# Weight preparation in an attention and expert-layer kernel: two sums drawn in the next chunk, squares drawn four places later

## The chip, the cores and the metric

The kernel runs on one core of one Trainium2 chip. The metric is the device time of one execution in microseconds (us). Before the change, three timed runs took 1914.98, 1915.31 and 1919.73 us; the median is 1915.31 us.

## The reference

Three layers follow one another; all inputs and the result are 32-bit in the reference, apart from what is noted below.

```python
# attention: 4 x 8 heads, 576 positions, head size 64, window 128
scores = q @ k.T / 8 + bias                  # bias = -slope_h * |i - j|, masked outside the window
x = softmax(scores) @ v                      # -> 2304 tokens x 512

# experts: 8 experts, 512 -> 1024 -> 512
P = exp(x @ w_gate - max)
for _ in range(8):                           # alternate row and column normalisation
    P /= P.sum(1, keepdims=True) + 1e-09
    P /= P.sum(0, keepdims=True) + 1e-09
    P *= 2304 / 8
x = sum(P[:, e:e+1] * (relu(x @ w1[e]) @ w2[e]) for e in range(8))

# last layer: 512 -> 2048 -> 512
h = x @ w_in                                 # w_in and w_out come as 64-bit floats
out = maximum(0.01 * h, h) @ w_out
```

## The kernel before

**Chunks and pairs.** Both expert layer and last layer are cut into chunks of 512 hidden columns: 16 chunks of the experts (0 to 15, two for each expert) and 4 of the last layer (16 to 19). The tokens are 18 tiles of 128, grouped into five pairs of token blocks (pairs 0 to 3 of two tiles a side, pair 4 of one). A unit is one chunk and one pair. From chunk 1 to chunk 18 the units of a chunk run in the order of pairs 0, 4, 1, 2, 3.

**Products.** A 2 x 2 block product is formed with seven products instead of eight (the list `PRODUCTS`), each of 16-bit high and low halves. A step is one such product: six matmuls of 256 columns (twelve of 128 for pair 4's first product). The first product of a unit (`a_steps`, matmuls at L728, "a") makes hidden values: ACT copies results out of the accumulation banks (L740, L752), DVE adds (L744, L757), ACT rounds to 16 bits (L776, L782, L798) and POOL forms the low halves (L801). The second product (`b_steps`, matmuls at L845, "b") takes them one unit later and adds onto the output tiles: DVE in one instruction (L858), or for two of the seven products ACT (L855) followed by POOL (L856). In the loop at L1031 the "a" steps of a unit are merged with the "b" steps of the unit before.

**Weights.** While a chunk runs, the weights of the next are prepared. `Weights` (L562) has one object for the first weights (`which` 0) and one for the second (`which` 1). `load` fetches 1024 KB on SP's queue into a buffer `raw`, of which there are two. `scale` squares the four quarters on ACT (L576, with sums), finds a power of two from them by small DVE and PE instructions (`scale_jobs`, L406), and scales the quarters on ACT (L579); for the second weights `back` (L588) follows. `part` (L605) splits a quarter into two 16-bit halves with ACT (L446) and POOL (L447). `sums` (L596) makes four sums and differences of quarters on POOL (L603). Parts 0 and 1 are taken before the sums; parts 2 to 6 need them (6 the third, 4 the fourth) and are made step by step in the last seven steps of the last "a" unit of a chunk (first weights) or of the "b" steps after it (second weights), by `at` (L621).

**Conversions.** In chunks 1 to 11 the list also holds the turning of the last layer's 64-bit weights into 32-bit ones, three conversions a chunk in chunks 1 to 10 and two in chunk 11 (`to_single`, L635). A conversion loads 512 KB into a `raw` buffer, and has five jobs: exponent (L657 DVE, L660 ACT), signed (L663 DVE), high (L668 DVE, L669 ACT), low (L675 ACT, L677 POOL) and put (L681 POOL, then a write of 256 KB, L682). The two `raw` buffers are taken in turn: first conversion, second conversion, first weights, third conversion, second weights. So the load of the first weights waits for the first conversion's write, and that of the second weights for the third conversion's write.

**The side list.** `side_jobs` (L1000) makes the list of these jobs for the next chunk; `None` is an empty place. It is begun with the unit of pair 4. After every step `tick` (L137) draws jobs from its head, as many as `-(-len(side) // max(len(seq) - k + rest, 1))` at step k, with `rest` 57, 36, 8 and -19 in the units of pairs 4, 1, 2 and 3. With the list of 85 jobs of a chunk with three conversions that is two jobs in each of the first seven steps and then one, and the list is empty before the end of pair 3. In pair 0's unit one job is drawn a step.

**What sets the order.** Jobs are drawn inside `tc.issue_after(...)` for each of the `anchors`: on its own engine a job's instruction must come behind the last evacuation that was recorded for that engine by the steps so far (`anchor`, L124). For the rest the planner of the tile framework (`schedule_with_timeline_sim=True`) orders the instructions of each engine ahead of time by place in the program and by when it takes their inputs to be there; on the chip each engine runs its own list in that order, and waits where an input is not there yet.

Of the kernel before, what the change touches and what calls it, by code (L numbers as in the profile page):

```python
# [31 lines left out]
def attn_moe_kernel(  # L32
# [80 lines left out]
    side, gating, inputs = [], [], []  # L113
# [337 lines left out]
    def weigh_pair(ci, p):  # L451
        t0, n = PAIRS[p]
        if ci not in pu:
            pu[ci] = small.tile([P, NTILE], F32, tag="pu", name="pu")
        c = slice(t0, t0 + 2 * n)
        nc.scalar.activation(out=pu[ci][:, c], in_=rxt[0 if ci == 0 else 1][:, c], func=AF.Copy, scale=rw[ci])

    class Inputs:
# [22 lines left out]
        def weigh(self):  # L481
            c = slice(self.t0, self.t0 + 2 * self.n)
            nc.scalar.activation(out=rxt[self.phase][:, c], in_=self.sr[:, 1:2].to_broadcast([P, 2 * self.n]), func=AF.Copy)
            if self.phase == 0:
                weigh_pair(0, self.p)
# [73 lines left out]
    W = [{}, {}]  # L559
    nw = [0, 0]  # L560

    class Weights:  # L562
# [52 lines left out]

        def early(self):
            if XTRA >= 2:
                return [lambda: self.part(0), lambda: self.part(1)] + [lambda k=k: self.sums(k) for k in range(4)]
            return []

        def at(self, j):  # L621
# [9 lines left out]
    def weights(ci):  # L631
        for which in range(2):
            W[which][ci] = Weights(ci, which)
# [366 lines left out]
    def side_jobs(ci, n):  # L1000

        todo = [to_single(cast.pop(0)) for _ in range(min(n, len(cast)))]
        weights(ci)
        a, b = W[0][ci], W[1][ci]
        jobs = [load for load, _ in todo[:2]]
        if not todo:
            return [a.load, b.load] + [None] * 10 + a.scale() + a.early() + b.scale() + b.early()
        jobs += [None] * 8 + todo[0][1] + [a.load]
        if len(todo) > 1:
            jobs += todo[1][1]  # L1010
        if len(todo) > 2:
            jobs += [todo[2][0]] + [None] * 4 + a.scale() + todo[2][1] + [b.load] + a.early()
        else:
            jobs += [b.load] + [None] * 8 + a.scale() + a.early()
        return jobs + [None] * 8 + b.scale() + b.early()
# [15 lines left out]
    for n, u in enumerate(units + [None]):  # L1031
        a, b = [], b_steps(*prev)
        if u == LAST:
            held_back = b[7:]
            b = b[:7]
        if u is None:
            b = held_back[:3] + [f for two in zip(b, held_back[3:] + [None] * 3) for f in two if f is not None]
        if u is not None:
            ci, p = u
            assert ci < NCE or p in split_pairs  # L1040
            a = a_steps(ci, p)
            k0 = len(a) - 7
            if p == ends[ci] and ci + 1 < NC:
                a = [[f] + ([lambda j=k - k0: W[0][ci + 1].at(j)] if k >= k0 else []) for k, f in enumerate(a)]
            else:
                a = [[f] for f in a]
        if prev[1] == ends[prev[0]] and prev[0] + 1 < NC:
            k0 = len(b) - 7
            b = [[f] + ([lambda j=k - k0: W[1][prev[0] + 1].at(j)] if k >= k0 else []) for k, f in enumerate(b)]
        else:  # L1050
            b = [[f] for f in b]
        if u is not None and ci >= 1:
            if n and units[n - 1][0] != ci and ci != NCE:
                weigh(ci)
            if p == 4:
                side += side_jobs(ci + 1, 3 if ci < NCE - 1 else 0) if ci + 1 < NC else []
        if prev[0] == NCE:
# [64 lines left out]
```

## Time and profile before

| What | Value |
|---|---|
| Median of three timed runs | 1915.31 us |
| The profiled execution | 1917.65 us |
| Its span | 1915.9 us |
| PE matmul busy | 1851.2 us (97%) |
| PE weight loads busy | 1609.8 us (84%) |
| ACT, POOL, DVE busy | 1363.5, 1325.1, 1312.1 us (71, 69, 68%) |
| DMA | 97.80 MB, nearly all on one queue (q1) |
| Load of 1024 KB of weights, median from issue to landing | 5.2 us |

PE multiplies, PEld loads its weights beside it, DVE, ACT and POOL are the other computing engines, SP issues the transfers. A row of the timeline gives the start in us, the duration in us, the engine, the line, the operation, what it writes and reads, its shape, and in brackets how long the engine was idle before it and what ended that. An idle time of an engine costs only when PE, or the end, waits for it.

### The profile page before, as it was taken

What the parts mean: (1) busy time and instruction counts of PE and PEld (TensorE: products, weight loads), DVE (VectorE), ACT (ScalarE), POOL (GpSimd) and SP (SyncE); (2) the same over time, 40 slices, a digit from 0 to 9 for tenths busy, and PEclk for the clock granted to TensorE, in tenths of its full rate; (3) what the DMA queues carried; (4) which work ended last, traced back from release to release, by engine and by line L of the source; (5) the groups of instructions that cost most, each with busy time, mean ns of one, the idle gap of its engine ahead of it and who ended that gap; (6) DMA issues with size and microseconds to landing.
All of it is one profiled execution on the core that took longest, in us unless ns stands there. A gap on an engine that the chain in (4) does not pass through costs nothing.

```text
span 1915.9 us, 45130 instructions
## 1 busy us (share of the span) xinstructions
PE 1851.2 (97%) x17725; PEld 1609.8 (84%) x17725; DVE 1312.1 (68%) x3608; ACT 1363.5 (71%) x3123; POOL 1325.1 (69%) x1140
## 2 busy tenths in 40 slices
PE   7899898999999999999999999999999998999999
PEld 5677787888888888988888888988889787889888
DVE  5455567766776767767676777666666687677877
ACT  7978767776767767676776767666665779776754
POOL 3843566877868686877868787685867786666753
PEclk8999999999999999999999999999999999999999
DMA  7522002021111202112111201100001010101002
GB/s 231 171 89 84 2 12 83 29 67 56 51 57 40 78 23 79 38 58 67 40 56 40 83 23 56 45 24 23 24 24 45 1 36 11 34 13 45 2 26 75
DMA packets 60453, 97.80 MB, mean 51 GB/s; under 512 B 3920, under 2 KB 26960, under 8 KB 60240
## 3 DMA queue, kind: packets, MB, share of 16 engines
q1 hardware_dynamic: 60240, 94.93, 15.4%
q8 instruction: 138, 2.26, 0.5%
q14 instruction: 75, 0.61, 0.1%
HBM read 81.81 MB, written 13.11 MB: 50 GB/s over the span
## 4 chain that ended last, share of the span: by engine, by line
PE 77%; ACT 10%; DMA 4%; DVE 4%; POOL 2%; issue 2%; SPq 0%; POOLq 0%; ACTq 0%; DVEq 0%
PE t L845 36%; PE s L728 21%; PE sq L728 15%; DMA raw<-in_moe_w_dram 3%; ACT e L261 2%; ACT junk L576 2%; PE o L305 1%; ACT raw L579 1%; PE pt L288 1%; DVE s L757 1%; ACT w L446 1%; PE s L249 1%; POOL h L801 1%; ACT xp L446 1%; ACT pb L292 1%
## 5 line engine op out<-in xcount | busy, mean ns | idle before, releaser
L845 PE MATMUL t<-w,h 128*128 128x256 f16 x7560 | 977.8, 273 | 15.1 <-DVE acc L858 5.3
L728 PEld LDWEIGHTS <-w 128*128 128x128 f16 x8400 | 758.5, 98 | 110.6 <-issue 28.6
L845 PEld LDWEIGHTS <-h 128*128 128x128 f16 x7560 | 729.5, 98 | 111.6 <-issue 24.2
L728 PE MATMUL s<-xp,w 128*128 128x256 f16 (+1 forms) x4872 | 611.6, 262 | 18.3 <-ACT q L752 11.4
L858 DVE SCALAR_TENSOR_TENSOR acc<-t,pu,acc 128x256 f32<-128x256 f32 x866 | 408.6, 478 | 207.9 <-PE t L845 160.0
L801 POOL TENSOR_TENSOR h<-s,h 128x1024 f16<-128x1024 f32 x180 | 389.0, 2161 | 120.1 <-ACT h L798 81.9
L728 PE MATMUL sq<-xp,w 128*128 128x256 f16 (+1 forms) x3528 | 451.1, 262 | 2.9 <-DVE s L757 2.6
L856 POOL TENSOR_TENSOR acc<-acc,part 128x256 f32<-128x256 f32 x322 | 234.7, 731 | 281.3 <-ACT part L855 246.4
L447 POOL TENSOR_TENSOR w<-raw,w 128x512 f16<-128x512 f32 x240 | 278.4, 1170 | 46.5 <-ACT w L446 46.2
L757 DVE SCALAR_TENSOR_TENSOR h<-sq,h 128x512 f16<-128x512 f32 (+1 forms) x352 | 192.8, 552 | 87.8 <-ACT h L782 49.3
L855 ACT ACTIVATE part<-t,pu 128x256 f32<-128x256 f32 x322 | 151.9, 472 | 100.8 <-PE t L845 95.1
L798 ACT ACTIVATE h<-s 128x1024 f16<-128x1024 f32 x180 | 189.7, 1054 | 43.4 <-DVE s L757 42.0
L744 DVE SCALAR_TENSOR_TENSOR sq<-sq,q 128x256 f32<-128x256 f32 x352 | 150.2, 427 | 60.3 <-PE sq L728 52.8
L740 ACT ACTIVATE q<-s 128x256 f32<-128x256 f32 x364 | 138.1, 381 | 70.3 <-PE s L728 57.1
L446 ACT ACTIVATE w<-raw 128x512 f16<-128x512 f32 x240 | 148.2, 628 | 8.9 <-PE t L845 6.6
L757 DVE SCALAR_TENSOR_TENSOR s<-sq,s 128x256 f32<-128x256 f32 x352 | 146.4, 416 | 2.0
L776 ACT ACTIVATE h<-sq 128x512 f16<-128x512 f32 x176 | 104.5, 594 | 59.3 <-PE t L845 30.1
L757 DVE SCALAR_TENSOR_TENSOR s<-sq,q 128x256 f32<-128x256 f32 x352 | 131.7, 415 | 13.4 <-ACT q L752 11.6
L744 DVE SCALAR_TENSOR_TENSOR sq<-s,q 128x256 f32<-128x256 f32 x176 | 75.4, 428 | 83.9 <-ACT q L740 78.8
L576 ACT ACTIVATE junk<-raw 128x512 bf16<-128x512 f32 x160 | 100.2, 626 | 44.2 <-DMA raw<-in_moe_w_dram 43.0
L782 ACT ACTIVATE h<-sq 128x256 f16<-128x256 f32 x176 | 66.8, 380 | 67.5 <-DVE sq L744 57.6
L579 ACT ACTIVATE raw<-raw,sr 128x512 f32<-128x512 f32 x160 | 102.4, 715 | 2.4 <-DVE sr L441 2.0
(142 smaller groups left out, 1713.0 us busy)
## 6 DMA issues: line engine op xcount, KB each, us to landing
raw<-in_moe_w_dram SPq DMA_DIRECT2D x32, 1024.0 KB, 5.2
k_t<-in_k_dram SPq DMA_DIRECT2D x16, 512.0 KB, 4.0
raw<-in_moe_w_in_dram SPq DMA_DIRECT2D x16, 512.0 KB, 3.6
raw<-in_moe_w_out_dram SPq DMA_DIRECT2D x16, 512.0 KB, 3.4
q_t<-in_q_dram SPq DMA_DIRECT2D x18, 256.0 KB, 4.1
v_t<-in_v_dram SPq DMA_DIRECT2D x18, 256.0 KB, 2.7
acc<-in_v_dram SPq DMA_DIRECT2D x18, 256.0 KB, 5.7
out_dram<-acc SPq DMA_DIRECT2D x36, 128.0 KB, 1.7
```

Source lines behind the costliest of these rows:

```text
L446: nc.scalar.activation(out=hi, in_=src, func=AF.Copy)
L447: return nc.gpsimd.tensor_tensor(out=lo, in0=src, in1=hi, op=ALU.subtract)
L576: nc.scalar.activation(out=junk, in_=self.raw[:, k], func=AF.Square, accum_out=self.mx[:, k:k + 1])
L728: nc.tensor.matmul(d[b][:, f, :], t[:, wp, kk, ft * P:(ft + 1) * P], XP[p][:, o, kk, xp, :], start=(i == 0 and f == 0 and j in FIRST), sto ...
L744: nc.vector.scalar_tensor_tensor(out=block(k), in0=ps, scalar=CS, in1=q[:, k], op0=ALU.mult, op1=ALU.add)
L757: nc.vector.scalar_tensor_tensor(out=out, in0=in0, scalar=sc, in1=in1, op0=op0, op1=op)
L798: nc.scalar.activation(out=h[:, 3:7, 0, :], in_=d["s"], func=AF.Copy)
L801: nc.gpsimd.tensor_tensor(out=h[:, 3:7, 1, :], in0=d["s"], in1=h[:, 3:7, 0, :], op=ALU.subtract)
L845: nc.tensor.matmul(ps, h[:, o, hp, f, tt * P:(tt + 1) * P], w[:, wp, ft, :], start=(i == 0 and j in FIRST), stop=(i == 5), skip_group_chec ...
L855: nc.scalar.activation(out=part, in_=ps, func=AF.Copy, scale=s)
L856: nc.gpsimd.tensor_tensor(out=dst, in0=dst, in1=part, op=ALU.add)
L858: nc.vector.scalar_tensor_tensor(out=dst, in0=ps, scalar=s, in1=dst, op0=ALU.mult, op1=ALU.add)
```

## The change

The third and fourth sums of the second weights leave the side list; they are put on the list anew at the unit of pair 0 of the chunk that uses these weights, behind one empty place each. And in a list with three conversions the empty places ahead of the first weights' `scale` (whose first jobs are the squares) are eight instead of four.

```diff
         def early(self):
             if XTRA >= 2:
-                return [lambda: self.part(0), lambda: self.part(1)] + [lambda k=k: self.sums(k) for k in range(4)]
+                return [lambda: self.part(0), lambda: self.part(1)] + [lambda k=k: self.sums(k) for k in range(4 - 2 * self.which)]
             return []
...
         if len(todo) > 2:
-            jobs += [todo[2][0]] + [None] * 4 + a.scale() + todo[2][1] + [b.load] + a.early()
+            jobs += [todo[2][0]] + [None] * 8 + a.scale() + todo[2][1] + [b.load] + a.early()
...
         if u is not None and ci >= 1:
             if n and units[n - 1][0] != ci and ci != NCE:
                 weigh(ci)
+            if p == 0:
+                side += [None, lambda w=W[1][ci]: w.sums(2), None, lambda w=W[1][ci]: w.sums(3)]
             if p == 4:
                 side += side_jobs(ci + 1, 3 if ci < NCE - 1 else 0) if ci + 1 < NC else []
```

## Rows read from the trace of the kernel before

**Rows 1.** The page, busy time, share of the span and instructions of each engine.
```profile
PE 1851.2 (97%) x17725; PEld 1609.8 (84%) x17725; DVE 1312.1 (68%) x3608; ACT 1363.5 (71%) x3123; POOL 1325.1 (69%) x1140
```

**Rows 2.** Stretches: length; PE, PEld, DVE, ACT, POOL busy; PE clock; DMA; GB/s.
```profile
347.20:1117.90 770.70, 758.41 (x7221) 670.77 (x7219) 546.80 (x1388) 544.10 (x1173) 591.04 (x496) 1.00 0.17 54
1117.90:1451.60 333.70, 333.70 (x3204) 297.62 (x3202) 221.66 (x586) 221.55 (x487) 239.12 (x204) 1.00 0.10 31
1451.60:1650.10 198.50, 185.75 (x1715) 159.37 (x1714) 140.56 (x391) 146.84 (x322) 140.79 (x115) 1.00 0.07 22
```

**Rows 3.** Waits over the span: who waited for whom, us, times, longest.
```profile
ACT junk L576 <- DMA raw<-in_moe_w_dram: 43.0, 22, 2.7
...
PE s L728 <- ACT q L752: 11.4, 13, 1.4
...
PE t L845 <- POOL h L801: 0.5, 2, 0.3
```

**Rows 4.** Timeline of chunk 9, around the first weights' load and squares.
```profile
981.40 0.86 DVE L858 SCALAR_TENSOR_TENSOR acc<-t,pu,acc 128x256 f32<-128x256 f32 x2
...
982.01 0.38 SPq L572 DMA_DIRECT2D raw<-in_moe_w_dram  x1
982.19 0.41 DVE L668 TENSOR_SCALAR raw<-raw 128x512 int32<-128x512 int32 x1
...
984.23 0.60 ACT L776 ACTIVATE h<-sq 128x512 f16<-128x512 f32 x1 [0.50 <-DVE sq L744]
...
987.20 0.63 ACT L576 ACTIVATE junk<-raw 128x512 bf16<-128x512 f32 x1 [2.38 <-DMA raw<-in_moe_w_dram]
...
989.82 0.38 ACT L752 ACTIVATE q<-s 128x256 f32<-128x256 f32 x1
...
990.25 1.70 PE L728 MATMUL s<-xp,w 128*128 128x256 f16 x12 [1.09 <-ACT q L752]
```

**Rows 5.** Timeline, ACT: the first squares in chunk 11 and in chunk 12.
```profile
1158.07 0.38 ACT L752 ACTIVATE q<-s 128x256 f32<-128x256 f32 x1
1160.05 0.63 ACT L576 ACTIVATE junk<-raw 128x512 bf16<-128x512 f32 x1 [1.60 <-DMA raw<-in_moe_w_dram]
...
1232.18 0.39 ACT L752 ACTIVATE q<-s 128x256 f32<-128x256 f32 x1
1232.45 0.64 ACT L576 ACTIVATE junk<-raw 128x512 bf16<-128x512 f32 x1
```

**Rows 6.** Timeline, POOL at the start of chunk 9: third and fourth sums, first later part.
```profile
952.60 1.28 POOL L603 TENSOR_TENSOR raw<-raw 128x512 f32<-128x512 f32 x1
953.83 1.43 POOL L856 TENSOR_TENSOR acc<-acc,part 128x256 f32<-128x256 f32 x2
955.20 1.29 POOL L603 TENSOR_TENSOR raw<-raw,t 128x512 f32<-128x512 f32 x1
...
962.26 1.16 POOL L447 TENSOR_TENSOR w<-t,w 128x512 f16<-128x512 f32 x1
```

**Rows 7.** Timeline of chunk 9: third conversion, second weights' load and first square.
```profile
1000.82 0.48 DVE L858 SCALAR_TENSOR_TENSOR acc<-t,pu,acc 128x256 f32<-128x256 f32 x1
...
1001.22 1.36 DVE L663 SCALAR_TENSOR_TENSOR raw<-raw,sign 128x512 int32<-128x512 int32 x1
...
1002.50 0.47 DVE L858 SCALAR_TENSOR_TENSOR acc<-t,pu,acc 128x256 f32<-128x256 f32 x1
...
1003.90 2.56 ACT L579 ACTIVATE raw<-raw,sr 128x512 f32<-128x512 f32 x4
...
1004.54 1.28 POOL L681 TENSOR_TENSOR raw<-raw 128x512 f32<-128x512 f32 x1
...
1007.95 0.38 SPq L572 DMA_DIRECT2D raw<-in_moe_w_dram  x1
...
1013.41 0.63 ACT L576 ACTIVATE junk<-raw 128x512 bf16<-128x512 f32 x1 [1.90 <-DMA raw<-in_moe_w_dram]
...
1014.04 0.36 ACT L740 ACTIVATE q<-sq 128x256 f32<-128x256 f32 x1
```

## The prediction, made before the changed kernel ran

> **What bounds the kernel now.** I read the busy line first: the matmul engine PE is busy 1851.2 of 1915.9 us, POOL, ACT and DVE about 70% of the span [rows 1]. So only PE's idle time, some 65 us, can be won, and anything new costs only what it makes PE wait. The table by stretches says where that idle time lies [rows 2]. In the nine chunks 2 to 10 (347.2 to 1117.9 us) PE is busy 758.41 of 770.70 us: 12.29 us idle, 1.37 us a chunk. In chunks 11 to 14 it is busy 333.70 of 333.70: nothing to win. In chunks 15 and 16, where the second layer's inputs are made, it is idle 198.50 - 185.75 = 12.75 us. The rest is attention, chunk 1 and the end. The granted clock is 1.00, the level of 2.4 GHz, in all three stretches, so it plays no part.
>
> Then the list of waits [rows 3]. PE's own largest is for ACT's copy L752: 11.4 us in 13 waits, at most 1.4. For POOL's h (L801) PE waits 0.5 us in the whole run: POOL is busy but no one that matters stands behind it. And ACT stands idle 43.0 us, 22 times, for a load of weights.
>
> The timeline of one chunk joins the two [rows 4]. The first weights' load is issued at 982.01. ACT finishes L776 at 984.83, and its next instruction in order is the first square (L576) of that load, which starts only at 987.20, when the load has landed, 5.19 us after its issue: ACT stands 2.38 us. Behind it are queued a copy of PE's product (L855), two more squares, L782 and L752; L752 runs at 989.82 and PE's next product starts at 990.25 after 1.09 us idle. That is the 1.37 us a chunk, nine times over (the small rest is one more short gap a chunk).
>
> **The change, part by part.** The sum is made on the profiled execution: 1917.65 us, of which the span is 1915.9; the three timed runs have a median of 1915.31, 2.3 us less, so I apply the sum to that.
>
> *Places.* In a chunk with three conversions the side list has 85 jobs; pair 4's unit draws two a step for 7 steps, then one a step. With four empty places more and two jobs fewer it has 87, and two are drawn in 9 steps. So the first conversion and the first weights' load stay (steps 5 to 7, and 7 instead of 8), the second conversion comes one to two steps earlier, and all from the first square on two steps later (step 19 becomes 21; a step is about 0.66 us of PE, so 1.3 us). Only these nine chunks (and chunk 1) have that list; in the others just the two sums leave it.
>
> *The squares, two steps later.* If place decided when they run, ACT's stand of 2.38 us would shrink by 1.3 us and L752 would be in front of them. Place does not decide here. A job is tied only behind the last evacuation, on its own engine, of the steps drawn so far, and the square drawn at step 19 of pair 4 runs behind L776 at 984.23, which belongs to pair 1 and stands eight or more steps later in the program [rows 4]. So it was passed over until the planner took its load for landed, which it seems to do about 2 us too early; two steps later in the program it would be passed over just as long. The load itself waits for the first conversion's write, which does not move. Where place does decide it looks different: in chunk 12, without conversions, the square runs right behind the L752 it is tied to, at 1232.45, with no stand at all [rows 5]. So I take 0. Bounds: -12.3 us (all idle time of the nine chunks gone) and, if ACT's stand stays but reaches one more evacuation, +1.37 a chunk, 12.3 us. The nearest row is row 4 itself, unchanged.
>
> *The third and fourth sums.* Eight sums a chunk of 1.28 us stay on POOL; none is added. In the program the two go from pair 3's steps 6 and 7 to steps 1 and 3 of the next chunk. But they run there already: nine chunks take 770.7 us [rows 2], 85.6 each, so chunk 9 begins near 347.2 + 7 x 85.6 = 946.6, and its two sums run at 952.60 and 955.20 [rows 6], since the load and scaling before them are late. What changes is that the two additions L856 between them (1.43 us) now stand ahead of the third sum. The third sum comes about 1.4 us later, the fourth hardly. What is next in need of them, the split of parts from the middle of pair 0's unit, starts only at 962.26 [rows 6], almost 6 us behind the fourth. Cost 0; the ends are 0 and the 2.55 us of two sums in each of 19 chunks, which would be 48 us if PE stood behind POOL, and PE's 0.5 us for L801 says that it does not. Nothing below 0 either, as PE is not waiting there.
>
> *What moves unasked: the second and third conversion.* Here place does decide. L663 of the third conversion runs at 1001.22, right behind the accumulation L858 of 1000.82 that it is tied to [rows 7]; so does L668 of the second (982.19, behind 981.40) [rows 4]. Two steps earlier, the second conversion's L668 is tied to an earlier accumulation, and its ACT and POOL parts and its write come up to a few us earlier. Nobody waits for those: 0. Two steps later, the third conversion's L668 and L669 fall behind the L858 of 1002.50: 1002.97 + 0.41 for L668 + about 0.63 for L669 (a pass over 512 columns, as a square) = 1004.0. Then POOL, free at 1004.54, does its two jobs of 1.28 us and ends at 1007.1 instead of 1005.82; if L669 falls behind the four scalings L579 (1003.90 to 1006.46), at 1006.46 + 0.63 + 2.56 = 1009.7. The second weights' load, now issued 2.1 us after that end (1007.95), goes 1.3 to 3.9 us later. Its squares stand ACT for 1.90 us at 1011.5 to 1013.4 [rows 7], and this stand moves with it. Today it costs PE nothing that I can find, and the stand of 1.60 us in chunk 11 costs nothing either (PE idle 0.00 there) [rows 2, 5]. In its new position it may meet a copy that PE needs, as the first does: from 0 to 1.37 us a chunk, 0 to 12.3 us. Two stands of three cost nothing; I take 0.1 us a chunk, 1 us.
>
> *Queues passed.* SP issues the same loads and writes; the second conversion's write and the third's load now go while the first weights' load (982.01 to 987.20) is under way. I take 0; the write is 256 KB, a quarter of that load, so at most a quarter of 5.19 us, 1.3 us a chunk.
>
> That last bound has a rule of the Trainium skill on its side: "DMA: Bandwidth & Descriptors", section "Issuing engines are not separate DMA queues", says that all transfers run on the same 16 DMA engines and interleave, by which the load would land late. The same page, "Queues, rings and completion order", has each engine take a ring's descriptors in ring order, by which a write issued later stays behind. No run here shows the two transfers together, so the first reading stays as a rival.
>
> *Chunks 1, 15 and 16.* The same POOL and ACT work in a slightly other order; their idle time is made of many single waits. I take 0, plus or minus 4 us, a third of the 12.75 us.
>
> Sum: 0 + 0 + 1 + 0 = +1 us: 1918.7 for a profiled execution, **1916 us** for the median. Its own range is 1910 to 1921.
>
> **Rivals.**
> 1. *Place decides after all (faster).* The squares run behind L752; ACT's first stand costs nothing, as in chunk 11, where L752 (1158.07) is ahead of the square (1160.05) [rows 5]. For it: in chunk 11 eight empty places lie between the load ahead and the squares, and PE has no idle time. Against it: in that chunk the load itself is later. 9 x 1.1 to 1.37 us = 10 to 12 us: 1903 to 1905.
> 2. *The second load's stand costs (slower).* It moves onto a copy such as L740, which now runs at 1014.04 [rows 7], directly after the first square. From about 1 us later on the square can stand ahead of a copy whose product is done, and PE's next product in that bank waits. 9 x 1 to 1.37 us = 9 to 12 us: 1924 to 1928.
> 3. *The first load lands late (slower)* because the earlier write shares its engines: 0.5 to 1.3 us more of ACT's stand, all of it PE's, in nine chunks: 1920 to 1927.
> 4. *Chance order in chunks 1, 15, 16* wins or loses more than 5.7 us: 1907 or 1923.
>
> **How the numbers follow.** A measurement of this kernel tells about 0.3%, 5.7 us, from no change: 1909.6 to 1921.0. Forecast 0.43. Rival 1: 0.18. Rival 2: 0.19. Rival 3: 0.05. Rival 4: 0.11 on the fast side and 0.04 on the slow side; there is more idle time to lose than work to add. So faster 0.29, same 0.43, slower 0.28. The range goes to the far sides of rivals 1 and 2: 1903.5 to 1927.
>
> **What would show it.** In chunks 2 to 10: ACT's first square again preceded by L776, with a stand near 2.4 us, and PE idle for L752 about 1.1 us (right); squares behind L752 or a stand below 1.2 us (wrong, rival 1). The second weights' load 1.3 to 3.9 us later in the chunk; the idle time of PE in 347.2 to 1117.9 still near 12.3 us, and a new wait of PE for L740 if rival 2 holds. The landing of the first load above 5.5 us would show rival 3. The third sums behind L856, with no wait of PE for POOL above 1 us in all. The prediction fails if the order on ACT around the squares changes at all.

## The result: 0.8% slower, and the profile after

The changed kernel takes 1932.97 us (median of 4 runs, 1932.21 to 1933.86), the kernel before 1915.14 us beside it (4 runs): 17.8 us more by these medians, 0.93%. The estimated ratio is 1.008 (95% interval 1.0068 to 1.0091), some 15 us, nearer to the 14.5 us by which the two profiled spans differ. The forecast was 1916 us, no change; the time lies above the range, which ended at 1927 us.

The profiled execution took 1932.21 us, its span is 1930.4 us, 14.5 us more than before. The page's busy line first: PE's work is the same 17,725 matmuls.

```profile
PE 1853.3 (96%) x17725; PEld 1608.5 (83%) x17725; DVE 1317.0 (68%) x3608; ACT 1357.2 (70%) x3123; POOL 1327.1 (69%) x1140
```

The table by stretches of the kernel after: chunks 2 to 10, 11 to 14, 15 and 16, and 18 (length; busy time of PE, PEld, DVE, ACT, POOL; granted clock; DMA share; GB/s):

```profile
343.30:1127.50 784.20, 762.98 (x7214) 670.98 (x7213) 549.23 (x1386) 538.79 (x1172) 592.88 (x496) 1.00 0.16 53
1127.50:1462.40 334.90, 334.73 (x3211) 298.40 (x3210) 223.39 (x588) 220.17 (x487) 239.36 (x205) 1.00 0.10 31
1462.40:1659.40 197.00, 184.90 (x1716) 159.61 (x1714) 142.13 (x391) 146.91 (x323) 141.21 (x115) 1.00 0.07 23
1740.60:1831.10 90.50, 86.80 (x822) 76.16 (x821) 64.63 (x173) 62.15 (x140) 56.85 (x50) 1.00 0.07 25
```

Chunk 18 in the kernel before, the same view:

```profile
1730.10:1815.40 85.30, 85.28 (x817) 75.68 (x815) 65.68 (x174) 62.69 (x143) 59.77 (x52) 1.00 0.08 26
```

Against [rows 2], chunks 2 to 10 grew from 770.7 to 784.2 us, 13.5 us, and chunk 18 from 85.3 to 90.5 us, 5.2 us. The rest moved by at most 1.5 us a stretch: chunks 11 to 14 +1.2, 15 and 16 -1.5, chunk 17 +1.3, chunk 19 -1.2. Attention and chunk 1 take some 4 us less together, but attention alone scatters by 4.8 us over the twenty kernels below, so this isn't put down to the change. The granted clock rounds to 1.00 in all four rows; it fell once within them, which is shown with the third place below.

The waits of the whole span in the kernel after, to set beside [rows 3]:

```profile
ACT junk L576 <- DMA raw<-in_moe_w_dram: 41.2, 22, 3.9
...
PE s L728 <- ACT q L752: 13.5, 26, 1.3
...
PE t L845 <- ACT part L855: 8.7, 13, 2.1
...
PE t L845 <- POOL h L801: 0.5, 2, 0.3
```

ACT stands no longer at the squares than before (41.2 against 43.0 us). What changed is how often PE is caught: waits for L752 went from 13 to 26. Within chunks 2 to 10 alone, PE's waits in the kernel before:

```profile
PE s L728 <- ACT q L752: 8.9, 9, 1.1
PE t L845 <- ACT part L855: 1.4, 3, 1.1
```

and in the kernel after:

```profile
PE s L728 <- ACT q L752: 12.1, 23, 1.3
PE t L845 <- ACT part L855: 7.1, 9, 2.1
```

One to four waits of PE a chunk, and only one in each of chunks 6 to 10, have become three to five. The timeline of the kernel after, in chunk 9 as in [rows 4] and [rows 7] (start, duration, engine, line, operation; in brackets idle time before it and what ended it):

```profile
987.81 0.38 SPq L572 DMA_DIRECT2D raw<-in_moe_w_dram  x1
...
991.11 0.47 ACT L855 ACTIVATE part<-t,pu 128x256 f32<-128x256 f32 x1
992.80 0.63 ACT L576 ACTIVATE junk<-raw 128x512 bf16<-128x512 f32 x1 [1.22 <-DMA raw<-in_moe_w_dram]
...
995.81 0.37 ACT L752 ACTIVATE q<-s 128x256 f32<-128x256 f32 x1
996.24 0.81 PE L728 MATMUL s<-xp,w 128*128 128x256 f16 x6 [0.53 <-ACT q L752]
...
1002.08 0.72 ACT L660 ACTIVATE raw<-raw,shift 128x512 int32<-128x512 int32 x1 [1.14 <-DVE raw L657]
1002.71 0.45 ACT L855 ACTIVATE part<-t,pu 128x256 f32<-128x256 f32 x1
...
1004.40 1.64 PE L728 MATMUL s<-xp,w 128*128 128x256 f16 x12 [0.38 <-ACT q L752]
...
1011.18 1.27 POOL L681 TENSOR_TENSOR raw<-raw 128x512 f32<-128x512 f32 x1
...
1016.57 0.38 SPq L572 DMA_DIRECT2D raw<-in_moe_w_dram  x1
...
1021.73 0.63 ACT L576 ACTIVATE junk<-raw 128x512 bf16<-128x512 f32 x1 [3.92 <-DMA raw<-in_moe_w_dram]
...
1024.20 0.45 ACT L855 ACTIVATE part<-t,pu 128x256 f32<-128x256 f32 x1
1024.71 1.31 PE L845 MATMUL t<-w,h 128*128 128x256 f16 x6 [2.08 <-ACT part L855]
```

Three places. First, the first weights' square now stands behind L855, not behind L776, for 1.22 us (0.81 to 2.00 us in chunks 4 to 10); PE loses 0.53 us here. Second, the third conversion's exponent L660 stands 1.14 us for DVE's L657, with L855 and L752 behind it; PE loses 0.38 us, in each of the chunks 4 to 10. Third, the second weights' load goes out 1016.57 - 951.9 = 64.7 us into its chunk (chunk 9 begins at 951.9) against 1007.95 - 947.6 = 60.4 us before; its square stands 3.92 us with L855 behind it, and PE loses 2.08 us. That is the longest of these chunks; in chunk 6 it is a stand of 2.20 us and two waits of PE, 0.36 us for L855 and 0.34 for L752.

Right behind that wait of 2.08 us the granted clock fell from 1.00 to 0.50, the level of 1.2 GHz, for 3.4 us. The stretch, in the form of the table above:

```profile
1024.88:1028.29 3.41, 3.41 (x18) 2.05 (x17) 2.71 (x12) 2.58 (x9) 2.51 (x3) 0.50 0.00 0
```

It cost some 1.7 us (an estimate: half of the 3.4 us), which stands in PE's busy time and not in its idle time.

The same reading of all nine chunks says what each place costs. I put each wait of PE down to the load whose landing it follows by less than 5 us:

| PE's waits in chunks 2 to 10 (us) | before | after |
|---|---|---|
| behind the first weights' load | 9.7 | 8.8 |
| behind the second weights' load | 0 | 7.6 |
| elsewhere | 1.9 | 3.9 |

Behind the second load PE waits in every one of the nine chunks: 0.56, 0.54, 1.22, 0.86, 0.70, 0.34, 0.72, 2.08 and 0.58 us. In the kernel before its square stood behind L798 with L740 next [rows 7]; now it stands behind L740 in chunks 3 to 10, and L855 and L752 come after it.

In chunk 12 the square still runs behind L752 without a stand, as in [rows 5]:

```profile
1242.88 0.38 ACT L752 ACTIVATE q<-s 128x256 f32<-128x256 f32 x1 [0.43 <-PE s L728]
1243.16 0.62 ACT L576 ACTIVATE junk<-raw 128x512 bf16<-128x512 f32 x1
```

POOL's third and fourth sums at the start of chunk 9, as in [rows 6], and the first later split on ACT that by the program's order reads one of them (part 4; the row holds part 5 as well), in the kernel after:

```profile
958.67 1.27 POOL L603 TENSOR_TENSOR raw<-raw,t 128x512 f32<-128x512 f32 x1
959.90 1.27 POOL L603 TENSOR_TENSOR raw<-raw 128x512 f32<-128x512 f32 x1
...
973.61 1.14 ACT L446 ACTIVATE w<-raw 128x512 f16<-128x512 f32 x2
```

and in the kernel before:

```profile
966.32 0.62 ACT L446 ACTIVATE w<-raw 128x512 f16<-128x512 f32 x1
```

Both sums are done 9.3 us into the chunk (8.9 us before), and that split starts at 21.7 us (18.7 before): here the sums are hidden as I said. (The sum that reads `t` is the third. In [rows 6] the fourth runs first, and the split `w<-t` at 962.26 is that of the second sum, which needs neither.)

In chunk 18 it is otherwise. In the kernel before, the same two sums ran in chunk 17 and were done 5 us before chunk 18 began at 1730.1; in the kernel after they run some 6 us into chunk 18, which begins at 1740.6. First before, then after:

```profile
1721.27 1.30 POOL L603 TENSOR_TENSOR raw<-raw 128x512 f32<-128x512 f32 x1
...
1723.62 1.29 POOL L603 TENSOR_TENSOR raw<-raw,t 128x512 f32<-128x512 f32 x1
```

```profile
1746.91 1.28 POOL L603 TENSOR_TENSOR raw<-raw,t 128x512 f32<-128x512 f32 x1
1748.14 1.27 POOL L603 TENSOR_TENSOR raw<-raw 128x512 f32<-128x512 f32 x1
```

PE's waits in chunk 18, which the kernel before has none of above 0.2 us, are for DVE.

```profile
1784.46 1.47 PE L845 MATMUL t<-w,h 128*128 128x256 f16 x12 [0.74 <-DVE acc L858]
...
1795.82 0.22 PE L421 MATMUL mt<-identb,e 128*1 128x128 bf16 x1 [0.83 <-DVE e L415]
```

### The profile page after: what moved, and what is told of

Read it like the earlier page. It is cut to its first block, busy times and chain, and to the rows that moved or that the text cites. A ratio compares the mean times of both kernels' runs of the same rounds, so it can differ in the third digit from the quotient of the medians.

```text
span 1930.4 us, 45138 instructions
## 1 busy us (share of the span) xinstructions
PE 1853.3 (96%) x17725; PEld 1608.5 (83%) x17725; DVE 1317.0 (68%) x3608; ACT 1357.2 (70%) x3123; POOL 1327.1 (69%) x1140
## 4 chain that ended last, share of the span: by engine, by line
PE 66%; ACT 11%; DMA 7%; POOL 6%; DVE 6%; issue 4%; SPq 0%; POOLq 0%; DVEq 0%; ACTq 0%
PE t L845 30%; PE s L728 18%; PE sq L728 13%; DMA raw<-in_moe_w_dram 6%; ACT junk L576 3%; POOL w L447 2%; DVE s L757 1%; ACT e L261 1%; PE o L305 1%; POOL acc L856 1%; DMA win<-raw 1%; DVE acc L858 1%; ACT h L798 1%; DVE h L757 1%; PE pt L288 1%
## 5 line engine op out<-in xcount | busy, mean ns | idle before, releaser
L845 PE MATMUL t<-w,h 128*128 128x256 f16 x7560 | 977.2, 273 | 22.9 <-ACT part L855 8.7
L728 PE MATMUL s<-xp,w 128*128 128x256 f16 (+1 forms) x4872 | 612.0, 262 | 19.5 <-ACT q L752 13.5
L858 DVE SCALAR_TENSOR_TENSOR acc<-t,pu,acc 128x256 f32<-128x256 f32 x866 | 406.1, 478 | 224.9 <-PE t L845 192.5
L801 POOL TENSOR_TENSOR h<-s,h 128x1024 f16<-128x1024 f32 x180 | 384.0, 2133 | 135.4 <-ACT h L798 105.2
L728 PE MATMUL sq<-xp,w 128*128 128x256 f16 (+1 forms) x3528 | 443.6, 262 | 3.3 <-DVE s L757 2.6
L856 POOL TENSOR_TENSOR acc<-acc,part 128x256 f32<-128x256 f32 x322 | 237.2, 738 | 267.4 <-ACT part L855 230.6
L757 DVE SCALAR_TENSOR_TENSOR h<-sq,h 128x512 f16<-128x512 f32 (+1 forms) x352 | 192.7, 552 | 76.2 <-ACT h L782 44.4
L855 ACT ACTIVATE part<-t,pu 128x256 f32<-128x256 f32 x322 | 151.7, 471 | 100.3 <-PE t L845 92.8
L740 ACT ACTIVATE q<-s 128x256 f32<-128x256 f32 x364 | 137.6, 380 | 112.5 <-PE s L728 89.5
L798 ACT ACTIVATE h<-s 128x1024 f16<-128x1024 f32 x180 | 189.7, 1054 | 38.1 <-DVE s L757 33.7
L757 DVE SCALAR_TENSOR_TENSOR s<-sq,s 128x256 f32<-128x256 f32 x352 | 146.2, 415 | 2.3
L757 DVE SCALAR_TENSOR_TENSOR s<-sq,q 128x256 f32<-128x256 f32 x352 | 131.8, 415 | 7.7 <-ACT q L752 5.7
L776 ACT ACTIVATE h<-sq 128x512 f16<-128x512 f32 x176 | 104.4, 593 | 41.8 <-DVE sq L744 28.5
L576 ACT ACTIVATE junk<-raw 128x512 bf16<-128x512 f32 x160 | 100.3, 627 | 42.8 <-DMA raw<-in_moe_w_dram 41.2
```

Source lines behind the costliest of these rows:

```text
L576: nc.scalar.activation(out=junk, in_=self.raw[:, k], func=AF.Square, accum_out=self.mx[:, k:k + 1])
L728: nc.tensor.matmul(d[b][:, f, :], t[:, wp, kk, ft * P:(ft + 1) * P], XP[p][:, o, kk, xp, :], start=(i == 0 and f == 0 and j in FIRST), sto ...
L757: nc.vector.scalar_tensor_tensor(out=out, in0=in0, scalar=sc, in1=in1, op0=op0, op1=op)
L798: nc.scalar.activation(out=h[:, 3:7, 0, :], in_=d["s"], func=AF.Copy)
L801: nc.gpsimd.tensor_tensor(out=h[:, 3:7, 1, :], in0=d["s"], in1=h[:, 3:7, 0, :], op=ALU.subtract)
L845: nc.tensor.matmul(ps, h[:, o, hp, f, tt * P:(tt + 1) * P], w[:, wp, ft, :], start=(i == 0 and j in FIRST), stop=(i == 5), skip_group_chec ...
```

## The experiments

The table gives for each kernel its time with the ratio to the kernel before on the same chip, and from its trace the length of chunks 2 to 10, that of chunks 17 to 19, and how long ACT stood at squares for a load within chunks 2 to 10. The kernel before took 1916.8 to 1918.3 us beside them (medians).

| kernel | us | ratio (95%) | chunks 2-10 | 17-19 | ACT's stand |
|---|---|---|---|---|---|
| before | 1915.1 | 1 | 770.7 | 262.1 | 37.7 |
| after | 1933.0 | 1.0080 (1.0068-1.0091) | 784.2 | 267.4 | 35.3 |
| sums_only | 1939.1 | 1.0110 (1.0095-1.0124) | 789.1 | 267.7 | 26.4 |
| places_only | 1944.0 | 1.0136 (1.0121-1.0151) | 798.1 | 262.1 | 28.7 |
| sums_held | 1943.4 | 1.0131 (1.0117-1.0144) | 792.4 | 267.1 | 24.6 |
| early_sums | 1928.6 | 1.0052 (1.0038-1.0066) | 782.0 | 262.1 | 26.0 |
| after_held | 1941.0 | 1.0123 (1.0107-1.0139) | 793.2 | 267.1 | 30.0 |
| before_const | 1918.3 | 1.0007 (0.9997-1.0017) | 771.1 | 262.1 | 0 |
| after_const | 1917.5 | 1.0000 (0.9991-1.0010) | 771.0 | 267.1 | 0 |
| sums_held_const | 1924.3 | 1.0033 (1.0023-1.0042) | 774.3 | 267.2 | 0 |
| places_const | 1921.6 | 1.0020 (1.0010-1.0030) | 777.6 | 262.1 | 0 |
| before_split | 1922.8 | 1.0030 (1.0021-1.0040) | 776.6 | 262.1 | 26.9 |
| after_split | 1929.2 | 1.0056 (1.0041-1.0071) | 778.7 | 267.1 | 14.2 |
| sums_held_split | 1934.1 | 1.0081 (1.0063-1.0099) | 784.0 | 267.1 | 24.7 |
| after_const_first | 1930.9 | 1.0067 (1.0050-1.0084) | 783.8 | 267.1 | 14.3 |
| after_const_second | 1922.4 | 1.0025 (1.0015-1.0036) | 773.7 | 267.1 | 14.3 |
| after_not18 | 1928.9 | 1.0059 (1.0044-1.0074) | 783.9 | 262.1 | 34.9 |
| conv_first | 1908.6 | 0.9951 (0.9936-0.9965) | 766.1 | 262.1 | 20.9 |
| change_conv_first | 1929.0 | 1.0063 (1.0045-1.0082) | 780.0 | 267.1 | 18.6 |
| conv_first_late | 1915.8 | 0.9996 (0.9986-1.0005) | 770.9 | 262.1 | 6.3 |

**The halves of the change.** Steps are counted from the list's end: with at most two jobs a step, a list of n jobs has its tail drawn one a step, so a job's late step is its index less (n - 78). Taking two jobs off the tail moves the jobs ahead of them two steps later; empty places move only what stands ahead of them, to earlier steps. sums_only is the change with

```diff
-            jobs += [todo[2][0]] + [None] * 8 + a.scale() + ...
+            jobs += [todo[2][0]] + [None] * 4 + a.scale() + ...
```

> One half of the change: the two sums move to the next chunk, the four empty places are not added, so the list of a three-conversion chunk has 83 jobs and everything in it, the first weights' load too, is drawn two steps later. Places theory (what costs is that the third conversion and the second weights' squares come two steps later): they still come two steps later here, so chunks 2 to 10 lose most of their 13.5 us and chunk 18 its 5.2 us: 1925 to 1933 us. Sums theory (what costs is the two sums in the next chunk, ahead of or between other work): as the whole change, 1930 to 1935. Chance theory (the planner finds another order at every small change, good or bad): anything from 1910 to 1935, with another pattern of PE's waits in chunks 2 to 10 than the changed kernel has.

1939.1 us, above the ranges of all three theories; chunks 2 to 10 at 789.1 us. places_only is the kernel before with that line the other way round (8 for 4).

> The other half: four more empty places ahead of the squares, all four sums where they were (list of 89 jobs). Steps are counted from the list's end here, so squares, third conversion and second load keep their steps; only the second conversion comes earlier. Places theory: chunks 2 to 10 within 4 us of before, 1911 to 1919 us. Sums theory: 1915 +- 2, since no sum moves. Chance theory: a difference of over 5 us either way in chunks 2 to 10 although no square and no third conversion moves in the program.

1944.0 us: the strongest surprise. In the program only jobs ahead of the empty places move: the second conversion (steps 8 to 10 in place of 9 to 13), with it the third conversion's load (10 for 14) and, against what I had expected, the first weights' load by one step (7 for 8). Chunks 2 to 10 take 27.4 us more. The places theory and the sums theory both fail here; only the chance theory had room for it.

sums_held moves the two sums and keeps every other job at its old step, by two empty places at the end of each list:

```diff
-        return jobs + [None] * 8 + b.scale() + b.early()
+        return jobs + [None] * 8 + b.scale() + b.early() + [None] * 2
```

> The two sums move to the next chunk, and two empty places take theirs at the end of every list, with the squares' four empty places as before: every other job is drawn at the step it had before. Places theory: PE's idle time in chunks 2 to 10 is back near 12 us; 1913 to 1921 us, the upper end if chunk 18 keeps its loss of 5 us. Sums theory: chunks 2 to 10 stay 10 to 14 us longer than before, 1928 to 1934 us. Chance theory: neither; another order of the squares on ACT than in either kernel.

1943.4 us, chunks 2 to 10 +21.7 us: more than the sums theory allowed, and nothing for the places theory. early_sums is the kernel before with the change's eight empty places and two jobs fewer, without a moved sum:

```diff
-   ... + [lambda k=k: self.sums(k) for k in range(4)]
+   ... + [lambda k=k: self.sums(k) for k in range(4 - 2 * self.which - self.which)] + (
+       [lambda: [self.sums(k) for k in (1, 2, 3)]] if self.which else [])
...
-   jobs += [todo[2][0]] + [None] * 4 + a.scale() + ...
+   jobs += [todo[2][0]] + [None] * 8 + a.scale() + ...
```

> The changed kernel's places without moving a sum: the second weights' sums 2 to 4 are one job at the end of the list instead of three, so the list has 87 jobs, the squares have their eight empty places, all from the first square on is drawn two steps later, and no sum is drawn in the next chunk. Places theory: chunks 2 to 10 lose 10 to 14 us as in the changed kernel, 1925 to 1930 us; chunk 18, without its moved sums, loses at most 2. Sums theory: 1913 to 1919 us. Chance theory: anything between, with waits at other places than the three of the changed kernel.

1928.6 us, chunks 2 to 10 +11.3 us and chunk 18 at 85.3 us, both as the places theory had it. So the places of the change without its moved sums cost 11.3 us, the sums alone 21.7, the empty places alone 27.4, and all together 13.5: the parts don't add. Chunks 2 to 10 of places_only:

```profile
346.66:1144.75 798.09, 762.64 (x7220) 671.04 (x7218) 557.31 (x1388) 539.91 (x1170) 593.19 (x497) 1.00 0.16 52
```

and sums_held:

```profile
346.69:1139.07 792.38, 764.14 (x7221) 672.52 (x7219) 550.52 (x1388) 541.94 (x1172) 590.78 (x497) 1.00 0.16 52
```

In these stretches PE idles 35.5 and 28.2 us, against 12.3 in [rows 2], with the same matmuls to do. after_held is the changed kernel with the two empty places of sums_held.

> The changed kernel with two empty places at the end of each list: squares and all after them are back at the steps of before; the second conversion comes earlier and the sums are in the next chunk. If the two steps that the squares move are what costs in chunks 2 to 10: those are back within 4 us of before, 1915 to 1923 us. If any new order costs as long as ACT stands at the loads: 1930 to 1950 us, like its two halves (places alone 1944, sums alone 1943).

1941.0 us: with the squares back at their old steps it is worse by 8 us (the end of the second conversion and the third conversion's load also come a step or two earlier than in the change). The two-step shift alone doesn't explain the cost; each new program gets another order from the planner, and each of these six orders costs.

**Is it ACT's stand?** In before_const and the three kernels like it the squares read a tile that is always there:

```diff
-   nc.scalar.activation(out=junk, in_=self.raw[:, k], func=AF.Square, accum_out=self.mx[:, k:k + 1])
+   nc.scalar.activation(out=junk.rearrange("p (a b) -> p a b", b=P), in_=ident.unsqueeze(1).to_broadcast([P, KT, P]),
+                        func=AF.Square, accum_out=self.mx[:, k:k + 1])
```

> The kernel before, but the squares that find a scale read a constant tile in SBUF in place of the freshly loaded weights (the scale is then not taken from the weights). ACT never stands at a square for a transfer. Stand theory (a new order costs PE because ACT stands 1 to 3 us in order for a load, with PE's copies queued behind it): PE's waits for L752 in chunks 2 to 10 go, 10 to 12 us less, 1903 to 1907 us. Order theory (each order that the planner makes has its own short waits, whatever stands): 1905 to 1930 us, as the new order falls.

> The changed kernel with squares of a constant tile (the scale is not taken from the weights). Stand theory: within 5 us of the kernel before with the same edit, some 8 us above it at most for chunk 18: 1905 to 1913 us. Order theory: still 8 to 20 us above the kernel before with the same edit, or below it, with PE's waits at other copies.

> Sums moved, all other jobs at their old steps, squares of a constant tile. Stand theory: the 22 us that this move costs chunks 2 to 10 go, 1905 to 1913 us (chunk 18 keeps 5 us). Order theory: still over 1920 us, with PE's waits for DVE's L757 and ACT's L752 and L855 in chunks 2 to 10 above 8 us.

> Only the four empty places more, squares of a constant tile. Stand theory: 1902 to 1910 us, the 27 us that the places cost in chunks 2 to 10 are gone. Order theory: still over 1920 us, since the second conversion's own waits remain.

1918.3, 1917.5, 1924.3 and 1921.6 us. All four lie above the ranges of the stand theory, and sums_held_const and places_const lie over 1920 us, as the order theory had it; in sums_held_const PE waits 13.6 us for L757, L855 and L752 in chunks 2 to 10, where the order theory had over 8. What speaks for the stand is the difference to before_const: in chunks 2 to 10 the cost of the change goes from 13.5 to 0.0 us, that of the moved sums from 21.7 to 3.2, that of the empty places from 27.4 to 6.5. So 76 to 100% of what these orders cost goes when the squares need not wait for the load, and the rest is other waits. The row of after_const, to set beside the 784.20 us above:

```profile
340.90:1111.95 771.05, 757.12 (x7220) 671.09 (x7218) 533.75 (x1387) 532.69 (x1173) 589.77 (x495) 1.00 0.17 54
```

The ranges of the stand theory fell with the first of them: before_const gained nothing (771.1 against 770.7 us) where 10 to 12 us were expected. PE's wait for L752, 8.9 us before, is 1.4 us there, but others have come, 5.1 us for ACT's part above all (the copies' lines are one higher in this kernel):

```profile
PE t L846 <- ACT part L856: 5.1, 8, 1.0
PE s L729 <- ACT q L741: 2.4, 3, 1.1
PE s L729 <- ACT q L753: 1.4, 3, 0.6
```

ACT hasn't stopped standing there either: it stands 22.1 us at the conversions' loads (L675 in the kernel before, where that was 2.4 us), and 12.8, 19.5 and 1.1 us in the other three.

A constant input also lets the planner place the squares otherwise, so the next kernels keep the dependency and shorten the wait: each load of 1 MB goes as four of 256 KB, one for each square.

```diff
-   nc.sync.dma_start(self.raw, chunks[...][...].rearrange("(k p) f -> p k f", p=P))
+   for k in range(KT):
+       nc.sync.dma_start(self.raw[:, k], chunks[...][...][k * P:(k + 1) * P])
```

> The kernel before, each load of weights issued as four transfers, one for each quarter of 256 KB that a square reads; nothing else. Stand theory: if the quarters land one after the other, the first is there some 1.3 to 2.5 us after its issue in place of 5.2 us (estimate: a quarter of the 5.19 us of [rows 4], and twice that), ACT's stand at the first square falls from 2.4 us to 0 to 0.5 us: -12 to 0 us, 1905 to 1917 us (the kernel before with squares of a constant gained nothing, so little is likely). If the four land together as late as the one: the time of before, 1918 +- 4, with the stand as before.

> The changed kernel with the loads of weights in four transfers; the squares read the loaded weights as in the kernel. Stand theory: ACT's stand at the squares falls under 0.8 us and with it the cost of the change, so within 6 us of the kernel before with the same split, 1910 to 1922 us. Dependency theory (the squares of a constant were cheap since the planner could place them anywhere, not since ACT did not stand): stays at 1929 to 1936 us though the stand is gone.

> Sums moved, all else at its old steps, loads of weights in four transfers. Stand theory: of the 25 us that this order costs over before, at least 12 go, as with squares of a constant (19 us): 1915 to 1931 us. Dependency theory: 1938 to 1946 us.

1922.8, 1929.2 and 1934.1 us. Against the kernel before with the same split, the change costs 2.1 us in chunks 2 to 10 (778.7 - 776.6) and the moved sums 7.4, a sixth and a third of their cost with whole loads, though ACT still stands 14.2 and 24.7 us. It is weaker than it looks. before_split itself lies above both its ranges (to 1917 and to 1922 us), as the split cost the kernel before 5.9 us there. after_split came 6.4 us above it, just outside the 6 us of the stand theory, and touches the dependency theory's 1929 to 1936 us. sums_held_split lies between the two theories' ranges. These three don't decide.

**Which load.** The constant tile for the first weights' squares only, then for the second's only (`if self.which == 0:` and `== 1:` ahead of the edit above), in the changed kernel:

> The changed kernel, the squares of the first weights of each chunk read a constant tile, those of the second read the loaded weights (the first scale is not taken from the weights). If the first load's stand carries the cost in chunks 2 to 10: 1917 to 1922 us, chunks 2 to 10 near 771 us. If the second load's stand does (my rival of the prediction): 1926 to 1933 us. If they share it by their waits in the changed kernel (PE waits 0.6 to 1.5 us at the first and 1 us at the second in a chunk): 1922 to 1927 us.

> The changed kernel, the squares of the second weights of each chunk read a constant tile, those of the first read the loaded weights. If the second load's stand carries the cost: 1917 to 1923 us. If the first's: 1928 to 1934 us. Shared: 1922 to 1928 us.

1930.9 and 1922.4 us. Chunks 2 to 10 go from 784.2 to 783.8 us with the first load's squares freed, to 773.7 us with the second's: 10.5 of the 13.5 us go with the second load's stand. 1930.9 us lies in the range of the second load alone; 1922.4 us lies in that range and in the one for a shared cost. Each of the two is a new order as well (in after_const_second PE waits 7.6 us for L740), so 10.5 is no exact price. The trace of the changed kernel says the same without a new order: 7.6 us of waits behind the second load, where after_const_second has none. The row of after_const_second:

```profile
342.75:1116.44 773.69, 758.44 (x7220) 671.17 (x7218) 544.65 (x1387) 536.99 (x1170) 593.61 (x497) 1.00 0.16 53
```

**Chunk 18.** In every kernel above with moved sums chunk 18 takes 90.5 us, in every one without 85.3. after_not18 leaves the sums of chunks 18 and 19 alone where they were:

```diff
-   range(4 - 2 * self.which)]
+   range(2 if self.which == 1 and self.ci < 18 else 4)]
...
-   if p == 0:
+   if p == 0 and ci < 18:
```

> The changed kernel, but the two sums of the second weights of chunks 18 and 19 stay where they were. If the moved sums cost the 5.2 us of chunk 18: chunk 18 at 85.3 us in place of 90.5, chunk 19 back at 96.9 (before) from 95.7, 1927 to 1930 us. If chunk 18 is longer for what came before it: 90.5 us still, 1931 to 1935 us.

1928.9 us, 4.0 less than the changed kernel, and the row of its chunk 18 is that of the kernel before:

```profile
1740.90:1826.20 85.30, 85.29 (x816) 75.66 (x815) 65.62 (x174) 62.64 (x143) 59.73 (x52) 1.00 0.08 26
```

Chunk 17 is back at 79.9 us and chunk 19 at 96.9. So moving the sums of these last two chunks costs 5.3 us in chunks 17 to 19.

**A program order that gives the loads time.** conv_first is the kernel before with the third conversion and the second weights' load ahead of the first weights' squares:

```diff
-   jobs += [todo[2][0]] + [None] * 4 + a.scale() + todo[2][1] + [b.load] + a.early()
+   jobs += [todo[2][0]] + [None] * 4 + todo[2][1] + [b.load] + a.scale() + a.early()
```

> The kernel before, with the third conversion and the second weights' load ahead of the first weights' squares in the program, so that both loads have more time until their squares. If a stand can be moved off the path by the program's order: ACT's stands at the squares fall under 25 us in all and PE's waits for L752 in chunks 2 to 10 with them, 1903 to 1912 us. If any new order brings new waits of PE: 1925 to 1945 us, as with the five orders tried so far.

1908.6 us, 0.49% faster than the kernel before (ratio 0.9951, 0.9936 to 0.9965), as its first theory had it; it beats both kernels. Its chunks 2 to 10:

```profile
343.62:1109.71 766.09, 756.41 (x7215) 671.11 (x7212) 542.19 (x1386) 541.93 (x1170) 586.35 (x496) 1.00 0.17 54
```

and the waits there, where ACT stood 37.7 us and PE waited 8.9 us for L752 before:

```profile
ACT junk L576 <- DMA raw<-in_moe_w_dram: 20.9, 17, 3.0
...
PE s L728 <- ACT q L752: 4.9, 8, 1.9
```

change_conv_first makes the same swap in the changed kernel; conv_first_late puts four of the eight empty places ahead of the second weights' squares between the second load and the first weights' squares.

> The changed kernel with the third conversion and the second weights' load ahead of the first weights' squares. If the cost of the change in chunks 2 to 10 is the second load's stand in its late place: chunks 2 to 10 within 4 us of the kernel before with this order (766 us), the whole 1908 to 1917 us, since the moved sums still cost some 4 us in chunks 17 to 19. If every new order has waits of its own: 1920 to 1935 us.

> The kernel before with the third conversion and the second load ahead of the first weights' squares, and these four steps later (four empty places from the second weights' squares put ahead of them). If the remaining stand of 1.4 us at the first squares costs PE 0.5 to 1.1 us a chunk: 1899 to 1906 us. If the later squares push the first weights' scaling into other work: 1909 to 1925 us.

1929.0 and 1915.8 us, both outside the range of the first theory and inside that of the second. In change_conv_first the squares' stand is as short as in conv_first (18.6 us), but now ACT stands at the conversions:

```profile
ACT raw L675 <- DMA raw<-in_moe_w_out_dram: 12.7, 7, 3.3
ACT raw L675 <- DMA raw<-in_moe_w_in_dram: 12.4, 7, 2.3
```

25.1 us for L675, which was 2.4 us in the kernel before, and 7.4 us in conv_first. In conv_first_late the squares stand only 6.3 us, and yet chunks 2 to 10 take 770.9 us:

```profile
ACT raw L675 <- DMA raw<-in_moe_w_out_dram: 8.4, 5, 2.1
...
ACT raw L675 <- DMA raw<-in_moe_w_in_dram: 8.2, 4, 2.6
ACT junk L576 <- DMA raw<-in_moe_w_dram: 6.3, 13, 1.3
```

The stand has gone over to the conversions' loads, 16.6 us of ACT's for L675. How long ACT stands in all doesn't give the time: at squares and L675 together it is 22.9 us here and 28.3 us in conv_first, which is 4.8 us shorter. What counts is whether copies that PE needs are behind a stand.

## Why the prediction was wrong

**What bounds the kernel** held in the main: PE has the same matmuls to do. Of the 13.5 us in chunks 2 to 10, 8.9 are idle time of PE (21.2 against 12.3 us), nearly all of it waits for copies on ACT. The other 4.6 lie in what the profile counts as busy: some 1.7 in the stretch at the lower clock, which I had said plays no part, and some 3 that I can't put down to a cause.

**"What moves unasked: the second and third conversion", taken at +1 us, is the term that failed.** Its mechanism was there. The second load left 1.2 to 4.3 us later in its chunk (4.3 in chunk 9), where I had 1.3 to 3.9, and its stand met copies that PE needs, L855 and L752. I priced it at 0.1 us a chunk since two of three stands cost nothing in the kernel before. It measured 0.34 to 2.08 us of PE's time in every chunk, 7.6 us in all, and its longest wait was followed by the lower clock; with the second weights' squares freed of their load 10.5 us go. That is my second rival, 9 to 12 us, to which I gave 0.19. Its place was a little off: I named L740 as the copy, it is L855 and L752. The second conversion, at 0, was misjudged as well: nobody waits for its result, but moving it earlier, with two loads beside it (places_only), cost 27.4 us.

**"The squares, two steps later: 0"** rested on the order on ACT staying as it was. It didn't: in chunks 4 to 10 L855 is ahead of the first square, not L776, and the stand there is shorter, 0.8 to 2.0 us for 2.2 to 2.7. Nor did the load stay in place: it leaves 1.4 to 1.7 us later in these chunks. I had written that the prediction fails if that order changes at all, and it did. PE's waits behind the first load went from 9.7 to 8.8 us, and freeing its squares wins only 0.4, so the 0 was nearly right in its amount, which was luck, and wrong in its reason.

**"The third and fourth sums: 0"** was right for the sums' own place in chunk 9: they run in the next chunk as before, hidden, and PE's wait for L801 is still 0.5 us. (I took the split at 962.26 for the first that needs them; it needs neither, so there was more room than I had counted.) It was wrong in two ways. "They run there already" was read from chunk 9 and doesn't hold for chunk 18, where the move is a real one: PE idles 3.7 us more there, and with chunk 17 and 19 the move costs 5.3 us, shown by after_not18. And with all other jobs held at their steps (sums_held) the move of two jobs that nobody waits for cost 21.7 us in chunks 2 to 10.

**Queues passed, rival 3: 0** was right. The first load still lands about 5 us after its issue (987.81, square at 992.80), though the second conversion's write is issued while it is under way, at 990.32.

**Rival 1, place decides after all,** is refuted: in chunks 3 to 10 the first square doesn't run behind L752 but ahead of it, and neither the old steps (sums_held, after_held) nor the new (early_sums) explain the time.

**Chunks 1, 15 and 16,** 0 within 4 us: they gave -1.2 and -1.5 us.

Behind all of these is one error of method. I moved one job at a time through an order that I held fixed. The order on ACT, DVE and POOL is made anew by the planner for each program. It seems to take loads as landed too early, as ACT stands up to 4.2 us at the squares; no run shows the planner's own times. In chunks 2 to 10, where ACT waits in order for a load of 5 us, a new order can put other copies behind the wait, as it did in the changed kernel. Of the ten changed programs here whose squares read whole loads, eight cost 9 to 27 us there, conv_first won 4.6 and conv_first_late came out even. In chunks 11 to 14, of which only chunk 11 has conversions, and two, no kernel here is more than 2.5 us from the time before.

What stays open: by which of its decisions the planner arrives at each order, so that no time of a new order could have been worked out from rows of the old one; why the later sums make PE wait for DVE in chunk 18 (L415 belongs to the scaling of the next weights and L858 to the output, not to the sums); and why the swap of conv_first doesn't help the changed kernel, beyond the 25.1 us at L675.

## What to carry to other kernels

Where a planner orders engines that run strictly in order, a small edit to the program must be priced as a new order: look at which transfers an engine will stand for, list the copies that can come to lie behind each, and take the range from that, not from the row that happens to be there now. Idle time that a profile shows as one wait a chunk can already be a favourable case of such an order, as here, where most new orders had more. A stand can be attacked by giving the transfer time in the program (the swap of conv_first won 0.49% in the kernel before and didn't save the changed one), and the result has to be measured, since the stand may go over to the next transfer.

## What the runs showed of the hardware

Four transfers of 256 KB don't land like four quarters of one. In before_split, one load in chunk 8:

```profile
812.70 1.75 SPq L573 DMA_DIRECT2D raw<-in_moe_w_dram  x4
...
815.26 0.63 ACT L577 ACTIVATE junk<-raw 128x512 bf16<-128x512 f32 x1 [0.94 <-DMA raw<-in_moe_w_dram]
...
816.50 0.63 ACT L577 ACTIVATE junk<-raw 128x512 bf16<-128x512 f32 x1 [0.51 <-DMA raw<-in_moe_w_dram]
...
819.25 0.63 ACT L577 ACTIVATE junk<-raw 128x512 bf16<-128x512 f32 x1 [0.47 <-DMA raw<-in_moe_w_dram]
```

The first quarter is there 2.56 us after the first issue, half of the 5.19 us of [rows 4] and not a quarter of it, and the last 6.55 us after, later than the whole load. Over chunks 2 to 10 of before_split the first quarter lands 2.5 to 3.2 us after the first issue and the last 4.8 to 6.6, where a whole load in the kernel before takes 4.9 to 5.5. Issuing four takes SP's queue 1.75 us where one takes 0.38.

The granted clock can fall behind one wait of PE. In chunks 2 to 10 it fell to 0.50 in ten of the twenty kernels, once or twice in each, and each time PE had waited 1.4 to 3.0 us in one piece shortly before (2.08 us in the row above at 1024.71). In the kernel before, whose longest wait there is 1.1 us, it didn't fall. No limit can be read from this: in after_const_second PE waited 2.1 us without a fall.
